# One attention-and-two-MLPs kernel: how the first MLP's input weights are kept, and the order of its opening

## The chip, the cores and the metric

The kernel runs on 1 core of one Trainium2 chip. The metric is the device time of one execution in microseconds (us). Three runs of the kernel before gave 1560.64, 1558.98 and 1560.36 us; the median is 1560.36 us.

## The reference

Two attentions follow each other for each of 8 batches and 8 heads (sequence 576, head dimension 64, 32 packed queries `p`), and then two MLPs work on all 4608 tokens (width 512, hidden width 2048):

```python
p_packed = sm_attn(p, k, v)            # softmax(scale * p k^T) v : 32 rows a head
x = sm_attn(q, p_packed, p_packed)     # 576 rows a head
x = x.transpose(0, 2, 1, 3).reshape(B * S, H * D)          # 4608 x 512
h = x @ w_in;   x = (h * sigmoid(h)) @ w_out               # first MLP (SiLU)
h = x @ w_in2;  x = (h * clip(h + 3, 0, 6) / 6) @ w_out2   # second MLP
```

The weights arrive as float64, q, k, v and p as float32 and the result is float32.

## The kernel before

**Products.** Each fp32 operand of the big products is split into a high word (rounded to the fast fp32r format) and a low word (the rest), and a product is made of three matmuls: high by high, high by low, low by high. A split is two instructions: a rounding copy on ScalarE and a subtraction on VectorE or GpSimd.

**Stages.** The first 512 tokens of a batch make one block, and the last 64 tokens of all eight batches (the "tails") make a ninth. An opening (lines 1567 to 1728, an order written out by hand, function by function) does the attention of batch 0 in two head groups n = 0 and 1, and converts the first weights. Block 0 then runs the first MLP on batch 0 while all of w_in and w_out is converted. Blocks 1 to 7 do the first MLP of the other batches: there w_in is not used itself, but a product of it with the packed values ("fused" weights, `fuse_steps`, L634 to L688). Block 8 runs the first MLP on the tails with w_in itself. After that `Second` does the second MLP.

**Inside a block.** `hidden` (L866 to L872) makes 12 matmuls for one of 16 slices f of the hidden width, then SiLU on ScalarE; `split_g` splits the result (L877 on ScalarE, L878 on VectorE); `project` makes 12 more matmuls two slices later. Between these, a planner (`Plan`) places attention steps and fused products: each has a place (a share of the block), a cost and waiting times, counted in ticks; a matmul is one tick, and in block 0 waiting times are multiplied by 1.5. Each engine and each DMA queue works strictly in the order of the program.

**Conversion of float64 (`conv_a` to `conv_lo`).** A piece of weights (128 x 512 numbers, 512 KB as float64) is loaded to `raw`. `conv_a` (L174, ScalarE) scales the upper half words into a `ring` tile; `conv_b` (L180, ScalarE) scales the lower half words into a second ring tile; `conv_shift` (L189) and `conv_sign` (L193) work on VectorE, `conv_add` (L202) on GpSimd. `conv_hi` (L213, ScalarE) and `conv_lo` (L218, VectorE) split the fp32 value. `Feed` does this for 32 pieces in turn, two for each slice f of block 0; loads in block 0 are issued from ScalarE's queue. The class `Prep` does the same in blocks 1 to 8 for the second MLP's weights (L318 to L336).

**Where w_in goes.** `keep` (L209, SyncE's queue) stores both words of each w_in piece in DRAM (`w1i`, 512 KB a piece, 16 pieces) and the odd pieces of w_out (`w1o`). `next_in` (L241, L243) loads w1i back, 512 KB at a time, 80 times: 64 times for fused products (L645 to L647) and 16 times for block 8. Five tiles `wi` rotate, so a load is issued when the piece five before it has been used.

**Tails of x in block 0.** `step_ut` (L563) transposes the last 64 columns of the weights `d2` on VectorE, `step_xt` (L585) multiplies them, and `flush` stores the result. Both head groups' steps stand in the plan of block 0 at place 0.02, `step_ut` right ahead of its `step_xt`, 12 ticks between the groups.

Of the kernel before, what the change touches and what calls it, by code (L numbers as in the profile page):

```python
# [18 lines left out]
def tile_pack_attention_two_mlps(ctx: ExitStack, tc, q, k, v, p, w_in1, w_out1, w_in2, w_out2, out):  # L19
# [13 lines left out]
    P = 128  # L33
# [93 lines left out]

    GF = T // P
    NG = NF // GF
    w1i = [dram.tile([KC, P, 2, GF, P], F32, name=f"w1i{g}", tag=f"w1i{g}") for g in range(NG)]  # L130
    w1o = {f: dram.tile([2, P, DM], F32, name=f"w1o{f}", tag=f"w1o{f}") for f in range(1, NF, 2)}
    WO = 3
    made = {}
# [40 lines left out]
        nc.scalar.mul(out=r, in_=f32(raw[:, :, 1]), mul=2.0 ** -112)  # L174
        raws[key] = raw, r.bitcast(I32)

    def conv_b(key, room=ring):
        raw, r = raws.pop(key)
        t = room().bitcast(I32)
        nc.scalar.mul(out=t, in_=raw[:, :, 0].bitcast(U32), mul=2.0 ** -29)  # L180
        raws[key] = raw[:, :, 1], r, t

    def conv_begin(key, room=ring):
        conv_a(key, room)
        conv_b(key, room)
# [30 lines left out]
    def conv_lo(key):  # L216
        (kind, f), v, w = key, raws.pop(key), made[key]
        nc.vector.tensor_sub(out=w[:, 1], in0=v, in1=f32(w[:, 0]))  # L218
        if kind == "in":
            kept.append((piece_in(f), f32(w).rearrange("p n (c f) -> p n c f", c=KC)))  # L220
        elif f % 2:
            kept.append((w1o[f].rearrange("n p f -> p n f"), f32(w)))

# [2 lines left out]
        conv_lo(key)  # L226

    def piece_in(f):
        return w1i[f // GF][:, :, :, f % GF, :].rearrange("c p n f -> p n c f")


    want_in, want_out = [], []
    have_in, have_out = {}, {}

    def next_in():
        if want_in:
            key = want_in.pop(0)
            t = wts.tile([P, 2, DM], F32R, tag="wi", name="wi", bufs=5)
            if len(key) == 3:
                j, g, c = key  # L240
                nc.sync.dma_start(out=f32(t).rearrange("p n (i f) -> p n i f", i=GF), in_=w1i[g][c])  # L241
            else:
                nc.sync.dma_start(out=f32(t).rearrange("p n (c f) -> p n c f", c=KC), in_=piece_in(key[1]))  # L243
            have_in[key] = t

    projected = [-1, -1]

# [15 lines left out]
    class Prep:  # L263
# [6 lines left out]
            self.steps = self.all()  # L270

        def room(self):
            return self.pool.tile([P, T], F32, tag="pring", name="pr", bufs=4)

        def load(self, u):

# [302 lines left out]
    def step_xt(n):  # L579
        pf = st.pop(("pp", n))  # L580
        a = st.pop(("a2t", n))
        b = n // QPB
        ps = bank()
        for j in range(2):
            mm(ps[:, j * TAIL:(j + 1) * TAIL], lhsT=pair(pf, j), rhs=a, start=True, stop=True)  # L585
        t = half_kb(n, "xt")[:, 0:2 * TAIL] if n == 1 else at.tile([P, 2 * TAIL], F32, tag="xt", name="xt")
# [49 lines left out]
    def fuse_steps(b, g):  # L636

        ms = mates[b]
        steps = []

        def product(ps, j, qd, first, last):
            lh, ll = [t[:, j * P:(j + 1) * P] for t in st["lp", b, qd]]
            w = have_in[b, g, 2 * qd + j]
            rh, rl = w[:, 0], w[:, 1]
            mm(ps, lhsT=lh, rhs=rh, start=first, stop=False)  # L645
            mm(ps, lhsT=lh, rhs=rl, start=False, stop=False)
            mm(ps, lhsT=ll, rhs=rh, start=False, stop=last)  # L647
# [201 lines left out]

    def hidden(j, f, tick, nxt):  # L850
        if j in (0, B):
            w = made.pop(("in", f)) if j == 0 else have_in[j, f]
            parts = [(w[:, 0, c * P:(c + 1) * P], w[:, 1, c * P:(c + 1) * P], xh[c], xl[c]) for c in range(KC)]
        else:
            s = slice(f % GF * P, (f % GF + 1) * P)
# [707 lines left out]
    beside(load_p, 0)  # L1563
    beside(load_nat, 0, "k", 1)
    load_tail(0, "k")
    load_tail(0, "q")
    beside(load_nat, 1, "k", 0)
    load_p(1)
    load_tail(1, "k")
    load_nat(1, "k", 1)  # L1570
    load_tail(1, "q")
    feed.load()
    for n in range(QPB):
        for j in range(2):
            load_nat(n, "v", j)
        load_tail(n, "v")
        for j in range(2):
            load_nat(n, "q", j)
        if n == 0:
            feed.load()  # L1580
    for _ in range(4):
        feed.load()
    load_p(2)
    load_tail(2, "k")
# [21 lines left out]
    a_qt(0)
    a_kp(1)
    a_qtc(0, "A")
    a_trc("k", 1, 1, "V")
    exp1(0)  # L1610
    a_tr("k", 1, 0)
    a_kpc(1, "V")
    conv_a(unit[0])
    a_tt(0)
    a_trc("k", 1, 0, "V")
    a_t(0)
    a_ttc(0, "A")
    conv_b(unit[0])
    a_s(1, 0)
    a_tc(0, "V")  # L1620
# [10 lines left out]
    a_max(1)
    a_tr("q", 0, 0)
    conv_hi(unit[0])
    a_ppf(0)
    a_tr("q", 0, 1)
    exp1(1)
    a_trc("q", 0, 0, "V")
    a_pt(0)
    a_trc("q", 0, 1, "A")
    post1(1)  # L1640
    a_tt(1)
    a_t(1)
    a_ttc(1, "V")
    a_ptc(0, "A")
    conv_shift(unit[1])
    conv_b(unit[1])
    a_z(0, 0)
    conv_sign(unit[1])
    a_tc(1, "A")
    a_z(0, 1)  # L1650
# [12 lines left out]
    a_tr("q", 1, 1)
    a_trc("q", 1, 0, "A")
    a_ph(0, "V")
    a_pt(1)
    a_trc("q", 1, 1, "A")
    conv_lo(unit[1])
# [62 lines left out]
    for j in range(NBLK):  # L1731
# [112 lines left out]
```

## Time and profile before

| what | value |
| --- | --- |
| median of three runs | 1560.36 us |
| the profiled execution's own time | 1563.44 us |
| its span, first to last instruction | 1561.7 us |
| TensorE busy | 1513.7 us (97%) |
| VectorE, ScalarE, GpSimd busy | 1045.4, 781.2, 193.5 us |
| mean granted TensorE clock | 0.989 of full speed |
| DMA, mean over the span | 230 GB/s |

How to read it: L12 is line 12 of the kernel; PE is TensorE, DVE VectorE, ACT ScalarE, POOL GpSimd, and SPq and ACTq are the queues in which SyncE and ScalarE issue DMAs. In a timeline row the first number is the start, the second the time to the end, both in us; in brackets stands how long the engine had been idle before it, and what released it. TensorE runs at one of two clock levels; a granted clock of 1.00 is 2.4 GHz, one of 0.50 is 1.2 GHz.

### The profile page before, as it was taken

The page shows a single profiled execution, that of the slowest core. Times are in us where ns is not written, and L with a number is a line of the kernel's source. Part 1 is how long each engine was busy: PE and PEld are TensorE (multiplying, and loading weights), DVE is VectorE, ACT ScalarE, POOL GpSimd, SP SyncE. Part 2 cuts the span into 40 slices and gives each one's busy share as a digit, 9 for nine tenths or more (in the row PEclk, how much of TensorE's full clock was granted, in tenths as well). Part 3 has the DMA queues.
Part 4 walks back from the last instruction along what each step waited for, and adds up shares of the span by engine and source line. Part 5 has one row for each costly group of instructions (what it writes and reads, how often), then busy time and mean ns, then how long its engine had stood idle before and what let it go on. Part 6 is the DMA issues. An engine that isn't in the chain of part 4 may idle for free.

```text
span 1561.7 us, 21728 instructions
## 1 busy us (share of the span) xinstructions
PE 1513.7 (97%) x7596; PEld 1234.8 (79%) x7596; DVE 1045.4 (67%) x1673; ACT 781.2 (50%) x1237; POOL 193.5 (12%) x173
## 2 busy tenths in 40 slices
PE   7899999999999999999999999999999999999997
PEld 4666766777777777778878888888888888999997
DVE  6677465755576455663362677877887777878776
ACT  5676545744566546655453334533443344444442
POOL 2333011111120111113132000000000000000000
PEclk9999999999999999999999999999999999999999
DMA  9899786987778776767597667677757776898886
GB/s 241 260 255 316 241 228 169 274 220 194 194 227 215 216 187 183 242 196 227 174 332 213 197 193 244 194 222 223 242 196 216 226 231 202 279 313 254 274 270 201
DMA packets 416460, 358.51 MB, mean 230 GB/s; under 512 B 155232, under 2 KB 307808, under 8 KB 416352
## 3 DMA queue, kind: packets, MB, share of 16 engines
q1 hardware_dynamic: 405552, 343.59, 73.7%
q10 hardware_dynamic: 10800, 13.54, 2.7%
q8 instruction: 61, 1.00, 0.3%
q14 instruction: 47, 0.39, 0.1%
HBM read 295.17 MB, written 61.87 MB: 229 GB/s over the span
## 4 chain that ended last, share of the span: by engine, by line
PE 85%; DMA 4%; DVE 3%; ACT 3%; SPq 2%; issue 1%; POOL 0%; ACTq 0%; POOLq 0%; DVEq 0%
PE acc L885 8%; PE b L1136 7%; PE b L1135 7%; PE b L1137 7%; PE b L1233 7%; PE b L1235 7%; PE b L1236 7%; PE acc L886 7%; PE acc L887 7%; PE hps L862 4%; PE hps L863 4%; PE hps L864 4%; PE abank L645 1%; PE abank L523 1%; PE abank L435 1%
## 5 line engine op out<-in xcount | busy, mean ns | idle before, releaser
L878 DVE TENSOR_TENSOR gl<-hps,gh 128x512 fp32r<-128x512 f32 x144 | 98.9, 687 | 171.5 <-ACT gh L877 170.6
L1235 PE MATMUL b<-ro,ws 128*128 128x512 f32 (+1 forms) x560 | 205.6, 367 | 0.0
L1135 PE MATMUL b<-xc,ws 128*128 128x512 f32 (+1 forms) x560 | 205.6, 367 | 0.0
L1137 PE MATMUL b<-xc,ws 128*128 128x512 f32 (+1 forms) x560 | 205.6, 367 | 0.0
L1136 PE MATMUL b<-xc,ws 128*128 128x512 f32 (+1 forms) x560 | 205.6, 367 | 0.0
L1236 PE MATMUL b<-ro,ws 128*128 128x512 f32 (+1 forms) x560 | 205.5, 367 | 0.0
L1178 DVE TENSOR_TENSOR ro<-g,ro 128x1024 fp32r<-128x1024 f32 (+1 forms) x140 | 161.3, 1157 | 42.7 <-ACT ro L1173 42.3
L1173 ACT CAST ro<-g 128x1024 fp32r<-128x1024 f32 (+1 forms) x140 | 132.9, 969 | 113.4 <-PE b L1233 46.7
L870 ACT ACTIVATE hps<-hps 128x512 f32<-128x512 f32 x144 | 84.0, 583 | 134.2 <-PE hps L864 131.4
L1233 PE MATMUL b<-ro,ws 128*128 128x512 f32 (+1 forms) x560 | 138.2, 368 | 0.6 <-DVE ro L1178 0.4
L885 PE MATMUL acc<-gh,wo 128*128 128x512 f32 x288 | 117.7, 409 | 1.3 <-ACT gh L877 1.3
L885 PE MATMUL acc<-gh,wr 128*128 128x512 f32 x288 | 117.4, 408 | 0.0
L1235 PEld LDWEIGHTS b<-ro,ws 128*128 128x128 f32 x560 | 105.1, 188 | 13.3 <-issue 0.2
L1136 PEld LDWEIGHTS b<-xc,ws 128*128 128x128 f32 x560 | 105.1, 188 | 13.2
L1135 PEld LDWEIGHTS b<-xc,ws 128*128 128x128 f32 x560 | 105.1, 188 | 13.2
L1236 PEld LDWEIGHTS b<-ro,ws 128*128 128x128 f32 x560 | 105.1, 188 | 13.1
L1137 PEld LDWEIGHTS b<-xc,ws 128*128 128x128 f32 x560 | 105.1, 188 | 13.1
L886 PE MATMUL acc<-gl,wo 128*128 128x512 f32 x288 | 114.0, 396 | 0.8 <-DVE gl L878 0.8
L1233 PEld LDWEIGHTS b<-ro,ws 128*128 128x128 f32 x560 | 102.4, 188 | 15.3 <-DVE ro L1178 2.4
L887 PE MATMUL acc<-gh,wo 128*128 128x512 f32 x288 | 113.7, 395 | 0.0
L887 PE MATMUL acc<-gh,wr 128*128 128x512 f32 x288 | 113.6, 394 | 0.0
L886 PE MATMUL acc<-gl,wr 128*128 128x512 f32 x288 | 113.4, 394 | 0.0
(295 smaller groups left out, 2928.4 us busy)
## 6 DMA issues: line engine op xcount, KB each, us to landing
ws<-w2in SPq DMA_DIRECT2D x280, 256.0 KB, 3.2
ws<-w2out SPq DMA_DIRECT2D x280, 256.0 KB, 3.4
wi<-w1i SPq DMA_DIRECT2D x80, 512.0 KB, 5.7
wo<-w1o SPq DMA_DIRECT2D x64, 512.0 KB, 5.5
x1d<-x SPq DMA_DIRECT2D x18, 512.0 KB, 7.1
w1i<-win SPq DMA_DIRECT2D x16, 512.0 KB, 7.4
praw<-in_moe_w_in_dram SPq DMA_DIRECT2D x32, 256.0 KB, 5.7
praw<-in_moe_w_out_dram SPq DMA_DIRECT2D x32, 256.0 KB, 5.2
```

The source lines that it names most:

```text
L878: nc.vector.tensor_sub(out=gl, in0=g, in1=f32(gh))
L885: mm(acc[e], lhsT=w[:, 0, s], rhs=gh, start=first, stop=False)
L886: mm(acc[e], lhsT=w[:, 0, s], rhs=gl, start=False, stop=False)
L887: mm(acc[e], lhsT=w[:, 1, s], rhs=gh, start=False, stop=last)
L1135: mm(ps, lhsT=wh, rhs=xs[k][:, 0, c], start=first, stop=False, skip_group_check=True)
L1136: mm(ps, lhsT=wh, rhs=xs[k][:, 1, c], start=False, stop=False, skip_group_check=True)
L1137: mm(ps, lhsT=wl, rhs=xs[k][:, 0, c], start=False, stop=last, skip_group_check=True)
L1173: nc.scalar.copy(out=t[:, 0], in_=v)
L1178: nc.vector.tensor_sub(out=t[:, 1], in0=self.operand(s), in1=f32(t[:, 0]))
L1233: mm(acc[i], lhsT=wh, rhs=ro[:, 1, f], start=False, stop=last, skip_group_check=True)
L1235: mm(acc[i], lhsT=wh, rhs=ro[:, 0, f], start=first, stop=False, skip_group_check=True)
L1236: mm(acc[i], lhsT=wl, rhs=ro[:, 0, f], start=False, stop=False, skip_group_check=True)
```

## The change

Five edits. (1) w_in pieces are stored unsplit: `w1i` holds one fp32 word for each number, 256 KB a piece. (2) `next_in` loads 256 KB and a new `split_in` splits a loaded tile with a copy on ScalarE and a subtraction on GpSimd, two loads later, or earlier if `piece` asks for it. (3) `conv_b` writes its result over the raw words instead of into a ring tile; `Prep`'s ring has 2 tiles instead of 4. (4) Block 0's tail steps are spread: `step_ut(0)` is the last step of the opening, `step_xt(0)` stands at place 0.05, `step_ut(1)` two (times 1.5) ticks later, `step_xt(1)` 20 (times 1.5) ticks after that, with a `flush` each. (5) The opening's loads and steps are reordered.

```diff
-    w1i = [dram.tile([KC, P, 2, GF, P], F32, ...) for g in range(NG)]
+    w1i = [dram.tile([KC, P, GF, P], F32, ...) for g in range(NG)]
...
-    def conv_b(key, room=ring):
+    def conv_b(key):
         raw, r = raws.pop(key)
-        t = room().bitcast(I32)
-        nc.scalar.mul(out=t, in_=raw[:, :, 0].bitcast(U32), mul=2.0 ** -29)
+        t = raw[:, :, 0]
+        nc.scalar.mul(out=t, in_=t.bitcast(U32), mul=2.0 ** -29)
         raws[key] = raw[:, :, 1], r, t
...
         if kind == "in":
-            kept.append((piece_in(f), f32(w).rearrange("p n (c f) -> p n c f", c=KC)))
+            kept.append((piece_in(f), v.rearrange("p (c f) -> p c f", c=KC)))
...
+    fresh = []
+
+    def split_in(behind):
+        while len(fresh) > behind:
+            t = have_in[fresh.pop(0)]
+            nc.scalar.copy(out=t[:, 0], in_=f32(t[:, 1]))
+            nc.gpsimd.tensor_sub(out=t[:, 1], in0=f32(t[:, 1]), in1=f32(t[:, 0]))

     def next_in():
...
-                nc.sync.dma_start(out=f32(t).rearrange("p n (i f) -> p n i f", i=GF), in_=w1i[g][c])
+                nc.sync.dma_start(out=f32(t[:, 1]).rearrange("p (i f) -> p i f", i=GF), in_=w1i[g][c])
...
             have_in[key] = t
+            fresh.append(key)
+        split_in(2)
+
+    def piece(*key):
+        if key in fresh:
+            split_in(len(fresh) - 1 - fresh.index(key))
+        return have_in[key]
...
-            w = have_in[b, g, 2 * qd + j]          # in fuse_steps
+            w = piece(b, g, 2 * qd + j)
...
-            w = made.pop(("in", f)) if j == 0 else have_in[j, f]          # in hidden
+            w = made.pop(("in", f)) if j == 0 else piece(j, f)
...
     load_tail(0, "k")
-    load_tail(0, "q")
     beside(load_nat, 1, "k", 0)
     load_p(1)
     load_tail(1, "k")
     load_nat(1, "k", 1)
-    load_tail(1, "q")
     feed.load()
     for n in range(QPB):
         for j in range(2):
             load_nat(n, "v", j)
         load_tail(n, "v")
+        load_tail(n, "q")
         for j in range(2):
             load_nat(n, "q", j)
-        if n == 0:
-            feed.load()
-    for _ in range(4):
+    for _ in range(5):
         feed.load()
...
-                plan.add(("xt", n), 0.02, 1, lambda n=n: [step_ut(n), step_xt(n)], [(("xt", m), 8) for m in range(n)], None, 5)
-            plan.add(("flush", 0), 0.02, 0, flush, [(("xt", QPB - 1), 8)])
+                if n:
+                    plan.add(("ut", n), 0.05, 0, lambda n=n: step_ut(n), [(("xt", n - 1), 2)])
+                plan.add(("xt", n), 0.05, 1, lambda n=n: step_xt(n), [(("ut", n), 20), (("flush", n - 1), 10)] if n else [], None, 5)
+                plan.add(("flush", n), 0.05, 0, flush, [(("xt", n), 10)])
```

The opening's new order, one step after the other (each is a function of the kernel before; "A" is ScalarE, "V" VectorE; u0 to u5 are the first six pieces: in0, in1, in2, out0, in3, out1). Before, `conv_a(u1)` stood ahead of `exp1(1)` and `conv_hi(u1)` ahead of `a_zmax(0)`, group 0 was carried through `exp1`, `a_t` and `a_pp` before group 1's scores, `a_sub(0)` was on GpSimd and `a_mul(1)` on VectorE.

```
a_s(1,0) a_trc(k,1,1,A) conv_sign(u0) exp1(0) a_s(1,1) conv_add(u0) post1(0) a_st(1) a_d(1,A) a_tt(0) a_dt(1,A)
conv_hi(u0) a_t(0) a_ttc(0,V) a_max(1) a_qt(0) a_tc(0,A) a_tr(q,0,1) conv_lo(u0) exp1(1) a_pp(0) a_trc(q,0,1,V)
... a_pp(1) a_z(0,1) a_ppf(1) conv_a(u1) conv_b(u1) a_zt(0) ... exp2(0) a_z(1,0) conv_shift(u1) conv_a(u2) a_sum(0)
... conv_a(u3) a_ztc(1) a_zmax(1) conv_a(u4) ... conv_b(u3) a_u(0) exp2(1) ... conv_sign(u1) a_x(0,0) ... conv_lo(u1)
... a_xl(3) conv_b(u4) conv_shift(u2) conv_sign(u2) conv_shift(u3) conv_add(u2) conv_sign(u3) conv_hi(u2) conv_lo(u2) step_ut(0)
```

## Rows read from the trace of the kernel before

**Rows 1.** First part of the page: engine, busy us (share), instructions.
```profile
PE 1513.7 (97%) x7596; PEld 1234.8 (79%) x7596; DVE 1045.4 (67%) x1673; ACT 781.2 (50%) x1237; POOL 193.5 (12%) x173
```

**Rows 2.** Windows view: stretch, length, busy per engine, granted clock, DMA share, GB/s.
```profile
80.00:90.00 10.00, 7.16 (x67) 5.21 (x66) 7.66 (x13) 8.81 (x16) 4.22 (x3) 1.00 0.79 230
...
120.00:140.00 20.00, 16.32 (x106) 12.78 (x105) 13.44 (x25) 14.09 (x28) 5.57 (x5) 0.91 0.98 317
...
800.00:850.00 50.00, 47.87 (x204) 38.89 (x203) 19.69 (x41) 24.12 (x41) 17.78 (x15) 0.97 0.99 294
...
50.00:53.40 3.40, 3.40 (x12) 2.92 (x12) 0.00 (x0) 1.77 (x4) 0.68 (x1) 0.50 0.17 38
...
256.00:336.00 80.00, 73.83 (x399) 53.95 (x398) 53.66 (x103) 50.19 (x87) 12.77 (x14) 0.98 0.84 237
432.00:508.00 76.00, 74.20 (x371) 56.15 (x370) 55.22 (x103) 48.13 (x84) 11.49 (x12) 1.00 0.79 226
```

**Rows 3.** Waits of TensorE, whole run: us in total, times, longest.
```profile
PE abank L507 <- DVE ppf L497: 5.5, 3, 2.3
PE abank L585 <- DVE a2t L563: 5.4, 3, 3.9
```

**Rows 4.** Timeline of the opening: SyncE's queue, ScalarE, TensorE.
```profile
13.04 0.98 SPq L149 DMA_DIRECT2D raw<-in_moe_w_in_dram  x1
...
18.01 0.66 ACT L174 ACTIVATE cr<-raw 128x512 f32<-128x512 f32 x1 [2.65 <-DMA raw<-in_moe_w_in_dram]
...
19.08 0.77 ACT L454 ACTIVATE spare<-spare,s1m 128x576 f32<-128x576 f32 x1
...
38.58 0.40 PE L862 MATMUL hps<-xh,win 128*128 128x512 f32 x1
```

**Rows 5.** Timeline of block 0's first slices: TensorE and VectorE.
```profile
42.18 0.66 PE L585 MATMUL abank<-a2t,ppf 128*128 128x64 f32 x4 [1.36 <-DVE a2t L563]
...
45.46 0.42 DVE L189 TENSOR_SCALAR cr<-cr 128x512 int32<-128x512 int32 x1
...
46.75 1.58 POOL L202 TENSOR_TENSOR cr<-cr 128x512 int32<-128x512 int32 x1 [3.36 <-DVE cr L193]
47.12 1.49 DVE L189 TENSOR_SCALAR cr<-cr 128x512 int32<-128x512 int32 x1
48.65 0.69 DVE L193 SCALAR_TENSOR_TENSOR cr<-raw,cr 128x512 int32<-128x512 int32 x1
...
49.55 0.73 PE L585 MATMUL abank<-a2t,ppf 128*128 128x64 f32 x4 [3.89 <-DVE a2t L563]
```

**Rows 6.** Groups view of 38 to 168 us, ScalarE: count, busy, mean ns, idle before.
```profile
L213 ACT CAST wr<-cr 128x512 fp32r<-128x512 f32 x8 | 5.0, 624 | 2.0 <-DMA w1i<-win 1.5 <-issue 0.4
L213 ACT CAST wo<-cr 128x512 fp32r<-128x512 f32 x8 | 4.9, 616 | 4.1 <-DMA w1o<-wo 2.7 <-DVE cr L193 0.8 <-POOL cr L202 0.6
```

**Rows 7.** Chain of waits in block 0: start, us, what.
```profile
114.21 10.00 DMA w1i<-win
```

**Rows 8.** DMA issues: out, in, queue, count, KB each, median us to landing.
```profile
wi<-w1i SPq DMA_DIRECT2D x80, 512.0 KB, 5.7
...
ws<-w2in SPq DMA_DIRECT2D x280, 256.0 KB, 3.2
```

**Rows 9.** Groups view, whole run, GpSimd: a low-word subtraction.
```profile
L330 POOL TENSOR_TENSOR c<-c,hi 128x640 fp32r<-128x640 f32 x32 | 50.6, 1580 | 0.0
```

**Rows 10.** Timeline at the end of block 1: SyncE's queue and ScalarE.
```profile
267.81 2.01 SPq L241 DMA_DIRECT2D wi<-w1i  x4
...
270.03 0.58 ACT L651 CAST xf<-abank 64x512 fp32r<-64x512 f32 x1
...
274.87 0.58 ACT L870 ACTIVATE hps<-hps 128x512 f32<-128x512 f32 x1
```

**Rows 11.** Timeline in block 8: ScalarE and GpSimd.
```profile
801.78 0.41 ACT L326 CAST hi<-c 128x256 fp32r<-128x256 f32 x1 [5.61 <-POOL c L318]
...
800.46 1.28 POOL L318 TENSOR_TENSOR c<-pr 128x512 int32<-128x512 int32 x1 [9.19 <-DMA w2out<-c]
```

More of the change, by code (lines that the diff above doesn't have):

```diff
@@ L129, in tile_pack_attention_two_mlps @@
     NG = NF // GF
-    w1i = [dram.tile([KC, P, 2, GF, P], F32, name=f"w1i{g}", tag=f"w1i{g}") for g in range(NG)]
+    w1i = [dram.tile([KC, P, GF, P], F32, name=f"w1i{g}", tag=f"w1i{g}") for g in range(NG)]
     w1o = {f: dram.tile([2, P, DM], F32, name=f"w1o{f}", tag=f"w1o{f}") for f in range(1, NF, 2)}
@@ L184, in conv_begin @@
         conv_a(key, room)
-        conv_b(key, room)
+        conv_b(key)
     def conv_shift(key):
@@ L228, in piece_in @@
     def piece_in(f):
-        return w1i[f // GF][:, :, :, f % GF, :].rearrange("c p n f -> p n c f")
+        return w1i[f // GF][:, :, f % GF, :].rearrange("c p f -> p c f")
     want_in, want_out = [], []
     have_in, have_out = {}, {}
+    fresh = []
[4 more added lines that the diff above has]
+            nc.gpsimd.tensor_sub(out=t[:, 1], in0=f32(t[:, 1]), in1=f32(t[:, 0]))
     def next_in():
@@ L240, in next_in @@
                 j, g, c = key
-                nc.sync.dma_start(out=f32(t).rearrange("p n (i f) -> p n i f", i=GF), in_=w1i[g][c])
+                nc.sync.dma_start(out=f32(t[:, 1]).rearrange("p (i f) -> p i f", i=GF), in_=w1i[g][c])
             else:
-                nc.sync.dma_start(out=f32(t).rearrange("p n (c f) -> p n c f", c=KC), in_=piece_in(key[1]))
+                nc.sync.dma_start(out=f32(t[:, 1]).rearrange("p (c f) -> p c f", c=KC), in_=piece_in(key[1]))
             have_in[key] = t
+            fresh.append(key)
[4 more added lines that the diff above has]
+        return have_in[key]
     projected = [-1, -1]
@@ L272, in room @@
         def room(self):
-            return self.pool.tile([P, T], F32, tag="pring", name="pr", bufs=4)
+            return self.pool.tile([P, T], F32, tag="pring", name="pr", bufs=2)
         def load(self, u):
@@ L585, in step_xt @@
             mm(ps[:, j * TAIL:(j + 1) * TAIL], lhsT=pair(pf, j), rhs=a, start=True, stop=True)
-        t = half_kb(n, "xt")[:, 0:2 * TAIL] if n == 1 else at.tile([P, 2 * TAIL], F32, tag="xt", name="xt")
+        t = at.tile([P, 2 * TAIL], F32, tag="xt", name="xt")
         copy_short(out=t, in_=ps[:, 0:2 * TAIL])
@@ L1588, in tile_pack_attention_two_mlps @@
     feed.load()
+    spread_p(0)
     turn_on(AF.Exp)
     a_tr("k", 0, 0)
-    spread_p(0)
+    a_trc("k", 0, 0, "A")
+    a_tr("k", 0, 1)
     a_kp(0)
-    a_trc("k", 0, 0, "V")
-    a_tr("k", 0, 1)
-    a_kpc(0, "V")
+    a_trc("k", 0, 1, "A")
+    a_tr("k", 1, 0)
+    a_kpc(0, "A")
+    spread_p(1)
     a_s(0, 0)
-    a_trc("k", 0, 1, "V")
-    spread_p(1)
+    a_trc("k", 1, 0, "V")
     a_s(0, 1)
+    a_kp(1)
+    a_d(0, "V")
+    conv_a(unit[0])
     a_st(0)
-    a_d(0, "A")
+    a_kpc(1, "A")
@@ L1603, in tile_pack_attention_two_mlps @@
+    conv_shift(unit[0])
     a_tr("k", 1, 1)
     a_dt(0, "A")
+    conv_b(unit[0])
     a_max(0)
[L1606 to L1609, printed above, removed]
+    a_s(1, 0)
+    a_trc("k", 1, 1, "A")
+    conv_sign(unit[0])
     exp1(0)
[L1611 to L1620, printed above, removed]
+    a_s(1, 1)
+    conv_add(unit[0])
     post1(0)
-    conv_shift(unit[0])
@@ L1623, in tile_pack_attention_two_mlps @@
-    a_s(1, 1)
-    conv_sign(unit[0])
     a_st(1)
     a_d(1, "A")
-    conv_add(unit[0])
-    a_pp(0)
-    a_dt(1, "A")
-    conv_a(unit[1])
[L1631 to L1645, printed above, removed]
-    conv_b(unit[1])
[L1647 to L1650, printed above, removed]
@@ L1651, in tile_pack_attention_two_mlps @@
-    conv_lo(unit[0])
-    conv_add(unit[1])
+    a_tt(0)
+    a_dt(1, "A")
+    conv_hi(unit[0])
+    a_t(0)
+    a_ttc(0, "V")
+    a_max(1)
+    a_qt(0)
+    a_tc(0, "A")
+    a_tr("q", 0, 1)
+    conv_lo(unit[0])
+    exp1(1)
+    a_pp(0)
+    a_trc("q", 0, 1, "V")
+    a_qtc(0, "A")
+    a_tt(1)
+    a_ppf(0)
+    a_tr("q", 0, 0)
+    a_ttc(1, "A")
+    post1(1)
+    a_pt(0)
+    a_trc("q", 0, 0, "A")
+    a_ph(0, "V")
+    a_t(1)
+    a_ptc(0, "V")
+    a_pl(0)
+    a_z(0, 0)
+    a_tc(1, "A")
@@ L1653, in tile_pack_attention_two_mlps @@
+    a_pp(1)
+    a_z(0, 1)
+    a_ppf(1)
+    conv_a(unit[1])
+    conv_b(unit[1])
     a_zt(0)
     a_zc(0)
-    a_pp(1)
-    conv_hi(unit[1])
+    a_pt(1)
+    a_tr("q", 1, 1)
     a_ztc(0)
+    a_ptc(1, "A")
     a_zmax(0)
-    conv_a(unit[2])
     a_tr("q", 1, 0)
-    a_ppf(1)
-    a_sub(0, nc.gpsimd)
-    a_tr("q", 1, 1)
+    a_trc("q", 1, 1, "A")
+    a_sub(0, nc.vector)
+    a_qt(1)
     a_trc("q", 1, 0, "A")
[L1665 to L1668, printed above, removed]
@@ L1669, in tile_pack_attention_two_mlps @@
-    a_qt(1)
-    a_ptc(1, "A")
     a_qtc(1, "V")
-    a_pl(0)
     exp2(0)
     a_z(1, 0)
-    conv_shift(unit[2])
-    a_ph(1, "A")
+    conv_shift(unit[1])
+    conv_a(unit[2])
     a_sum(0)
@@ L1679, in tile_pack_attention_two_mlps @@
     conv_b(unit[2])
-    a_pl(1)
-    spread_p(2)
     a_rec(0)
-    conv_a(unit[3])
     a_zt(1)
@@ L1686, in tile_pack_attention_two_mlps @@
     a_zc(1)
+    a_ph(1, "A")
     a_mul(0, nc.gpsimd)
-    conv_b(unit[3])
+    conv_a(unit[3])
     a_ztc(1)
     a_zmax(1)
-    conv_a(unit[5])
+    conv_a(unit[4])
+    a_pl(1)
+    spread_p(2)
     a_sub(1, nc.vector)
-    conv_b(unit[5])
+    conv_b(unit[3])
     a_u(0)
@@ L1700, in tile_pack_attention_two_mlps @@
     a_al(0)
-    conv_a(unit[4])
-    a_mul(1, nc.vector)
+    a_mul(1, nc.gpsimd)
+    conv_a(unit[5])
+    conv_sign(unit[1])
     a_x(0, 0)
+    a_u(1)
     a_x(0, 1)
-    a_u(1)
+    conv_add(unit[1])
     a_xh(0)
+    a_ah(1)
     a_xl(0)
-    a_ah(1)
+    a_al(1)
+    conv_hi(unit[1])
     a_xh(1)
-    a_al(1)
-    conv_b(unit[4])
-    conv_sign(unit[2])
+    conv_lo(unit[1])
     a_x(1, 0)
@@ L1715, in tile_pack_attention_two_mlps @@
     a_x(1, 1)
-    conv_add(unit[2])
     a_xh(2)
@@ L1719, in tile_pack_attention_two_mlps @@
     a_xh(3)
+    conv_b(unit[5])
     a_xl(3)
+    conv_b(unit[4])
+    conv_shift(unit[2])
+    conv_sign(unit[2])
+    conv_shift(unit[3])
+    conv_add(unit[2])
+    conv_sign(unit[3])
     conv_hi(unit[2])
     conv_lo(unit[2])
-    conv_shift(unit[3])
-    conv_sign(unit[3])
+    step_ut(0)
     feed.begun, feed.ended, feed.at = 6, 3, 4
```

## The prediction

> **What bounds the kernel.** I read the first part of the page, then the windows, then TensorE's waits, and then the timeline wherever a window showed TensorE idle. TensorE is busy for 1513.7 us of a span of 1561.7 [rows 1], so 48 us of idle time, and what the lower clock costs, are all that this change can touch: it adds and removes no product of the two MLPs. The reader should see that the loss sits in a few places. One is the opening, ahead of the first product of block 0 at 38.58 [rows 4]. One is block 0: 2.8 us idle in 80 to 90 and 3.7 in 120 to 140, where the granted clock also falls to 0.91 of 20 us, 1.8 us more [rows 2]. One is the stretch 256 to 336, with 6.2 us idle, while 432 to 508 loses only 1.8 [rows 2]. One is block 8, with 2.1 us idle in 800 to 850 and 1.5 us of clock [rows 2]. By name, the waits that the change touches directly are those for the transposed tails, 5.4 us in three, 1.36 and 3.89 of it in block 0 [rows 3, 5]. After the long one the clock stands at 0.50 for 3.4 us, which costs 1.7 us [rows 2].
>
> The sum is made against the profiled execution, 1563.44 us, which is its span and 1.7 us around it. The median of the runs shown, 1560.36, lies 3.1 lower, so 3.1 comes off at the end.
>
> **A, the opening.** ScalarE stands 2.65 us waiting for the second raw piece, issued at 13.04 and in use at 18.01, and group 1's exponential starts only at 19.08 behind it and one rounding copy [rows 4]. In the new order nothing of that piece stands ahead of this exponential; I lay the new chain out (score copies, u0's conversion, exponential of group 0, copy of its transpose) and reach about 16.5, 2.6 us earlier. But the piece's load moves behind all of v and q. With the 5.0 us from issue to use of [rows 4] and an issue near 16.5 it is ready at 21.5, just where ScalarE now wants it, and its two passes still stand ahead of `exp2(0)`. Two q tails leave the front of SyncE's queue, which brings u0 about 1.2 us sooner and leaves q's landing about where it was. I keep 1.6 us of the 2.6: the first product at 37.0. Bounds: 3 us gained, 1 us lost. Moving `a_sub(0)` and `a_mul(1)` between engines lies inside this.
>
> **B, the tails.** `step_ut(1)` went onto VectorE behind a shift of 1.49 us and a sign step of 0.69 [rows 5], and TensorE stood in `step_xt` until it came. With 30 ticks between the two (30 matmuls of 512 columns are 6.4 us at 2.4 GHz, an estimate from the clock) the second wait is gone. For the first: VectorE ends x near 38.5, then come shift, sign, shift beside GpSimd's addition, sign, low word and transposition, 0.42 + 0.69 + 1.49 + 0.69 + 0.7 + 0.2 = 4.2 us (the low word taken like the sign step, the transposition from the end of that step to TensorE's start) [rows 5], so 42.7. TensorE comes to `step_xt(0)` after 21 matmuls, 4.5 us at 2.4 GHz and some gaps, so at 41.8. Of 5.25 us about 1.0 stays: 4.2 gained. A wait of that size left the clock alone before, so the 1.7 us go too. B is -5.9; bounds -7 and 0. What is late next are the pieces in2, out0 and in3; in2's low word is ready about 1.5 us before it is wanted, so I see no new stall at once.
>
> **C, the rest of block 0.** What is lost there is 2.8 + 3.7 + 1.8, and about 1.7 if the clock also falls after the first: 10 us. At its root VectorE is late with `ppf` (two of the three waits in [rows 3]), after ScalarE had waited 1.5 and 2.7 us for stores to free their tiles [rows 6]; one store of w1i took 10 us [rows 7]. These stores halve, 16 times 256 KB less, and the five reloads in block 0 halve too. Against it, TensorE asks for pieces 7.5 us sooner, `raw` is freed by GpSimd's addition instead of VectorE's sign step, and a ring tile is now held until its store lands. Bounds: -10 and +6; I take -3.5, about one of the two waits. The conversion in place takes no instruction away and I cost it at nothing: the strided read on GpSimd is the unknown, hidden while GpSimd is busy 4 to 6 of 10 to 20 us [rows 2]; if GpSimd's additions took half as long again, `conv_hi` would come 0.7 us later, inside C's bounds.
>
> **D, the end of block 1.** Four fused products follow each other and ScalarE has no gap until SiLU at 274.87 [rows 10]. Each step now adds a split: a copy of 0.62 us [rows 6], 2.5 for four. The last two splits want tiles of the four loads issued from 267.81 on [rows 10]; behind the third step's casts and two copies ScalarE comes to the first of them at 271.8. By 3.2 us from issue to landing it is there, by 5.7 it costs 1.7 us [rows 8]; I take 1.5. ScalarE's queue holds SiLU and the copies that free the accumulators behind this, so TensorE waits for all of it: +4.0. Bounds +2.5 and +8 (both waits at full, and a clock drop).
>
> **E, the other reloads.** 60 copies of 0.62 us are 37 us of ScalarE, and 60 subtractions on GpSimd at 512/640 of 1.58 us [rows 9] are 76. ScalarE is busy 63% of those stretches and TensorE idle 5% [rows 2]. If a copy costs TensorE only where it already waits, that is 1.9 us; I take +2. Bounds 0 and +12: a split waits in ScalarE's queue for a tile issued only two steps before, and every SiLU behind it waits too.
>
> **F, block 8.** GpSimd waits 9.19 us for a store to land and ScalarE 5.61 us for GpSimd [rows 11], at 0.99 DMA share [rows 2]. Eleven reloads there halve; against it come 16 copies. I take -1; bounds -3.6 and +3.
>
> Sum: -1.6 - 5.9 - 3.5 + 4.0 + 2.0 - 1.0 = -6.0, so 1557.4, and 1554.3 on the scale of the median.
>
> **The rivals.**
> 1, slower: ScalarE's queue blocks on landings. It decides if a 256 KB reload still takes the 5.7 us that 512 KB took [rows 8], since a tile is split two fused steps after its load is issued, and where the steps come in a bunch, as the four loads in 2 us of [rows 10] show, that is less time than it takes. D becomes 8, E 12, C nothing: -7.5 + 8 + 12 = +12.5, so 1572.9 - 3.1 = 1569.8. For it: the boundary's gapless ScalarE. Against it: 3.2 us for `ws`.
> 2, handed back: block 0 ends when its feed ends. A and B's 7.5 us turn into waits for conversions, so +1.5: 1561.8. For it: ScalarE busy 8.81 and VectorE 7.66 of 10 us [rows 2]. Against it: 14.09 and 13.44 of 20 later.
> 3, the traffic was the root: all of C and F go. -1.6 - 5.9 - 10 + 4 + 2 - 3.6 = -15.1: 1545.2. For it: rows 7 and 11. Against it: ScalarE and VectorE remain loaded.
> 4, GpSimd's added subtractions hold VectorE up. The same shift takes 0.42 us alone and 1.49 beside GpSimd's addition [rows 5], 1.07 more; if VectorE is held up in the critical spot at six of the 80 reloads, 6.4 us: 1560.7. Against it: VectorE has a third of its time free in 256 to 336 [rows 2].
> The Trainium skill, "SBUF — State Buffer", section "SBUF: two separate sides", says that VectorE and GpSimd share one port pair as an exclusive lock, so that some VectorE operations block for a whole GpSimd instruction. The two shifts agree with it; by the rule alone each of the 80 subtractions could block one VectorE operation, and rival 4 would be the forecast.
>
> **Chances.** Forecast 0.48, rival 1 0.12, rival 2 0.17, rival 3 0.15, rival 4 0.08. A measurement of this kernel tells 0.2% (3.1 us) from no change, so faster means under 1557.2 and slower over 1563.5. Faster: 0.46 of the forecast, rival 3 and 0.02 of rival 4, 0.63. Same: 0.02 of the forecast, 0.12 of rival 2, 0.05 of rival 4, 0.19. Slower: rival 1, 0.05 of rival 2, 0.01 of rival 4, 0.18. The range 1543 to 1566 leaves out most of rival 1 and the edges. The likeliest case has 1549 to 1559 for itself.
>
> **What would show it.** A: the first product of block 0 near 37.0. B: no wait for `a2t` over 1.5 us before 60, and no 0.50 clock near 50. C: less idle between 70 and 140, shorter w1i stores. D: SiLU of block 2 some 4 us later after its last fused cast than before. E: idle ScalarE ended by "DMA wi"; none would sink rival 1. F: the clock at 808. The forecast is wrong if block 0 ends less than 5 us earlier than before, or if TensorE waits for `wi` splits in more than a few places.

## The result, and the profile after

The changed kernel takes 1567.75 us (median of 6 runs, 1564.85 to 1570.87) against 1559.67 for the kernel before in the same session. The ratio is 1.0054, 95% interval 1.004 to 1.0068: slower by 0.54%, some 8.4 us. 1554.3 was forecast, within 1543 to 1566; the time lies outside on the slow side. The profiled execution took 1568.68 us, with a span of 1566.9, 5.2 more than before.

The page's first part answers to [rows 1]: ScalarE gained 44 us, GpSimd 108, and VectorE 16.5, although it has four instructions fewer (the new order of the opening moves a few between the engines).

```profile
PE 1512.8 (97%) x7596; PEld 1231.4 (79%) x7596; DVE 1061.9 (68%) x1669; ACT 825.0 (53%) x1321; POOL 301.4 (19%) x253
```

TensorE's waits (us in total, times, longest), beside [rows 3]: the one for the tails' transposition shrank, the one for `ppf` grew, one for q's load stands in the list with 3.1 us, and four for splits are new, 3.7 us in all; the longest of them is shown.

```profile
PE abank L523 <- DVE ppf L513: 8.4, 4, 4.7
...
PE abank L432 <- DMA spare<-in_q_dram: 3.1, 2, 2.3
...
PE abank L601 <- DVE a2t L579: 2.4, 4, 1.8
...
PE hps L878 <- ACT wi L241: 1.7, 1, 1.7
```

The windows of [rows 2]: TensorE is busy for 14.75 us of 120 to 140 instead of 16.32, and for 72.42 of 256 to 336 instead of 73.83, while the DMA shares of these two stretches fell.

```profile
80.00:90.00 10.00, 7.54 (x34) 5.72 (x35) 9.78 (x16) 7.72 (x15) 3.76 (x3) 0.87 1.11 291
120.00:140.00 20.00, 14.75 (x95) 11.26 (x94) 15.98 (x22) 12.01 (x23) 10.85 (x8) 0.91 0.63 165
800.00:850.00 50.00, 46.49 (x200) 36.81 (x199) 24.52 (x43) 26.61 (x47) 28.69 (x22) 1.00 0.82 245
...
256.00:336.00 80.00, 72.42 (x384) 51.91 (x382) 51.52 (x99) 58.02 (x101) 31.72 (x29) 0.96 0.70 182
```

The timeline of the opening, SyncE's queue and TensorE, beside [rows 4]. SyncE issues two v loads at 13.27 and then nothing until 18.12: its next load, the v tail of group 1, needs the tile `vt` (one buffer), and group 0's products read that tile from 17.75. The q loads of group 1 stand behind it, TensorE waits 2.30 us for them, and the first product of block 0 comes at 41.00 instead of 38.58.

```profile
13.27 1.13 SPq L376 DMA_DIRECT2D spare<-in_v_dram  x2
18.12 0.63 SPq L366 DMA_DIRECT2D vt<-in_v_dram  x1
...
19.63 2.63 SPq L387 DMA_DIRECT2D spare<-in_q_dram  x4
...
17.75 0.32 PE L505 MATMUL abank<-vt,a1Tt 64*32 64x64 f32 x8
...
25.64 1.73 PE L432 MATMUL abank<-ident,spare 128*128 128x128 f32 x8 [2.30 <-DMA spare<-in_q_dram]
...
41.00 0.39 PE L878 MATMUL hps<-xh,win 128*128 128x512 f32 x1
```

Despite that start, block 0 is 4.5 us ahead of before at its twelfth slice (SiLU at 123.9 against 128.4). Then it loses all of it: the sixteenth is at 155.6 against 156.0. How large the lead was is uncertain, since single traces scatter: in that of e4 (below), which takes the time of the kernel before, these slices stand at 123.6 and 153.3, and against it the changed kernel goes from 0.3 us behind to 2.3. The timeline of VectorE and GpSimd shows the place, with the shift that takes 0.42 us when alone [rows 5]. Both lines on GpSimd, the new subtraction (L242) and the old addition (L202), have an instruction of VectorE beside them that takes 1.4 to 1.5 us, and the second of these is `ppf`, for which TensorE waits 4.7 us.

```profile
127.25 1.83 POOL L242 TENSOR_TENSOR wi<-wi 128x512 fp32r<-128x512 f32 x1 [1.64 <-ACT wi L241]
...
127.86 1.50 DVE L189 TENSOR_SCALAR cr<-cr 128x512 int32<-128x512 int32 x1
...
130.17 1.28 POOL L202 TENSOR_TENSOR cr<-cr,raw 128x512 int32<-128x512 int32 x1 [1.09 <-DMA raw<-in_moe_w_out_dram]
130.32 1.41 DVE L513 TENSOR_TENSOR ppf<-ppn,mask 128x256 f32<-128x256 f32 x1
```

At the end of block 1, beside [rows 10], four copies of 0.62 us stand between the casts, and SiLU begins at 279.11 instead of 274.87; from block 1's last SiLU that is 24.4 us instead of 21.8. A reload now takes 3.7 us from issue to landing, against 5.7 [rows 8].

```profile
269.20 4.04 SPq L250 DMA_DIRECT2D wi<-w1i  x4
...
270.09 0.62 ACT L241 CAST wi<-wi 128x512 fp32r<-128x512 f32 x1
...
279.11 0.58 ACT L886 ACTIVATE hps<-hps 128x512 f32<-128x512 f32 x1
```
```profile
wi<-w1i SPq DMA_DIRECT2D x80, 256.0 KB, 3.7
```

### The profile page after: what moved, and what is told of

It is laid out like the page before. It is cut to its first block, busy times and chain, and to the rows that moved or that the text cites. A ratio compares the mean times of both kernels' runs of the same rounds, so it can differ in the third digit from the quotient of the medians.

```text
span 1566.9 us, 22022 instructions
## 1 busy us (share of the span) xinstructions
PE 1512.8 (97%) x7596; PEld 1231.4 (79%) x7596; DVE 1061.9 (68%) x1669; ACT 825.0 (53%) x1321; POOL 301.4 (19%) x253
## 4 chain that ended last, share of the span: by engine, by line
PE 79%; ACT 6%; DVE 4%; DMA 4%; issue 3%; SPq 2%; POOL 1%; ACTq 0%; POOLq 0%; DVEq 0%
PE b L1249 7%; PE b L1251 7%; PE b L1252 7%; PE b L1151 7%; PE b L1153 7%; PE b L1152 7%; PE acc L901 7%; PE acc L902 6%; PE acc L903 6%; PE hps L878 4%; PE hps L880 4%; PE hps L879 4%; DMA ws<-w2in 1%; PE abank L451 1%; PE abank L661 1%
## 5 line engine op out<-in xcount | busy, mean ns | idle before, releaser
L242 POOL TENSOR_TENSOR wi<-wi 128x512 fp32r<-128x512 f32 x80 | 107.5, 1348 | 178.6 <-ACT wi L241 164.0
L1232 POOL TENSOR_TENSOR ov<-ov,o 128x1024 f32<-128x1024 f32 (+1 forms) x5 | 10.9, 2182 | 654.6 <-ACT ov L1218 654.6
L901 PE MATMUL acc<-gh,wr 128*128 128x512 f32 x288 | 117.3, 407 | 0.0
L901 PE MATMUL acc<-gh,wo 128*128 128x512 f32 x288 | 116.7, 405 | 0.4 <-ACT gh L893 0.4
```

What stands on the lines that cost most here:

```text
L242: nc.gpsimd.tensor_sub(out=t[:, 1], in0=f32(t[:, 1]), in1=f32(t[:, 0]))
L901: mm(acc[e], lhsT=w[:, 0, s], rhs=gh, start=first, stop=False)
```

## The experiments

Each was timed in five rounds against the kernel before on the same chip; ratios below 1 are faster. Microseconds are the ratio's distance from 1 times 1560. Where the trace times of two variants are compared, the reference is e4, which does the least. Differences of two single traces are good to some microseconds only: e1's last SiLU of block 8 comes 3.5 us ahead of e10's, although by the ratios e1 is 0.8 us slower.

**e1 to e4: one part of the change at a time, on the kernel before.**

```
e1: w1i unsplit, split_in, piece, conv_b in place   (everything else as before)
e2: + step_ut(0) after conv_lo(unit[2]); plan: ("ut", n), ("xt", n), ("flush", n)
e3: the new order of the opening and its loads
e4: conv_b in place, Prep's ring 4 -> 2
```

> The kernel before with the halved stores, the splits at the reload and the in-place low words alone; opening, loads and tails as before. Theory 1 (the splits cost the time): slower by 6 to 10 us, so a ratio near 1.005; SiLU of block 2 begins 3 to 5 us later than before, block 8 ends with another 2 to 4 us more, TensorE has waits ended by ACT wi and POOL wi. Rival (the new opening costs the time and the splits are hidden): within 2 us of before. Rival 3 of the prediction (halved traffic frees block 0): block 1 begins 3 us or more earlier than before.

> The kernel before with only the tails moved: the transposition of group 0's tail stands at the end of the opening, group 1's has a step of its own in the plan. Theory 1 (block 0 ends when its feed ends): 4 to 5 us earlier at block 0's first quarter, then handed back in waits for ppf, block 1 begins within 1 us of before, ratio 0.999 to 1.001. Rival (the feed was held up by the splits, the stores or the in-place low words in the changed kernel, not by its own pace): the 4 to 6 us stay, ratio 0.996 to 0.998.

> The kernel before with only the reordered opening and its loads; the tails are transposed where they were. Theory 1: the first product of block 0 comes 1.5 to 2.5 us later than before, as in the changed kernel, and what is left of it at the start of block 1 is 0 to 2 us, ratio 1.000 to 1.002. Rival (the late opening is made by the in-place low words or their effect on GpSimd): the first product at or before 38.6, as before.

> The kernel before with only the low words converted in place (raw tiles held until GpSimd's addition, half the ring tiles used, the second weights' ring halved). Theory 1: costs nothing, within 1 us of before. Rival (the strided operand slows GpSimd's additions or VectorE beside them): slower by 2 to 5 us, GpSimd's addition of block 0 longer than 1.58 us.

| | ratio | 95% | us |
|---|---|---|---|
| e1, split | 1.0053 | 1.0039 to 1.0066 | +8.3 |
| e2, tails | 0.9957 | 0.9944 to 0.9971 | -6.7 |
| e3, opening | 1.0049 | 1.0030 to 1.0067 | +7.6 |
| e4, in place | 0.9996 | 0.9985 to 1.0007 | -0.6 |

For e1 the splits' theory held in time; by the trace, SiLU of block 2 comes 2.9 us later than before and block 8 adds 1.35, both a little less than it asked for. Its third line, the prediction's rival 3, did not hold: block 1 began only 2.1 us earlier than before, and 0.6 later than in e4. For e2 the rival held: the gain stays, so block 0 is not bound by the pace of its feed. The window from 45 to 55 of e2, and of the kernel before, shows it: TensorE busy throughout at full clock, where it had 6.11 of 10 us at 0.83.

```profile
45.00:55.00 10.00, 10.00 (x49) 7.32 (x47) 9.38 (x14) 8.85 (x19) 5.33 (x4) 1.00 1.07 309
```
```profile
45.00:55.00 10.00, 6.11 (x26) 4.86 (x25) 5.74 (x10) 5.11 (x10) 2.84 (x2) 0.83 0.48 142
```

In e3 the first product came at 40.97, as expected, but I had expected 0 to 2 us to be left of it and 7.6 were. In its trace, that of an execution 5 us slower than its median, the waits for the tails, still in their old place, grew from 5.4 to 7.3 us. It has the same hole in SyncE's queue, 13.35 to 17.71. For e4 theory 1 held: nothing.

**e5 and e6: the opening without SyncE's wait.** e5 is the changed kernel with group 1's v tail in a tile of its own (one of the spares that the change had set free by taking group 1's `xt` out of it); e6 is the same without the reload split.

```
-        if n == 1 and what != "v":
+        if n == 1:
```

> The changed kernel, with one difference: the v tail of group 1 takes a tile of its own instead of waiting for that of group 0, so SyncE no longer stands at it with the loads of q behind it. Theory 1 (the opening is late because of that wait, 13.94 to 18.12 on SyncE): group 1's q lands near 21.5 instead of 25.5, the first product of block 0 comes 3 to 4 us earlier, ratio to the kernel before 1.002 to 1.004. Rival (ScalarE's copies in the new order set the opening): q lands earlier but the first product moves by less than 1 us, ratio 1.005.

> Tails moved, low words in place, new opening with the v tail of group 1 in a tile of its own; the reload split is left out, weights are stored and reloaded split as before. Theory 1: all that the splits cost is gone and the new opening, without SyncE's wait, is as good as the old: 1551 to 1553, ratio 0.994 to 0.997. Rival (the order itself is worse than the old one): 1555 or more, ratio above 0.997.

e5: 1563.03 us, ratio 1.0016 (1.0005 to 1.0028), against 1.0054 of the changed kernel: the wait was worth some 5.9 us, and theory 1 held, if just below its range. The timeline of e5's opening has the loads without a hole and the first product at 36.73.

```profile
12.10 1.13 SPq L376 DMA_DIRECT2D spare<-in_v_dram  x2
13.28 0.63 SPq L366 DMA_DIRECT2D spare<-in_v_dram  x1
13.95 0.62 SPq L366 DMA_DIRECT2D spare<-in_q_dram  x1
14.62 2.63 SPq L387 DMA_DIRECT2D spare<-in_q_dram  x4
...
36.73 0.40 PE L878 MATMUL hps<-xh,win 128*128 128x512 f32 x1
```

e6: 1553.0 us, ratio 0.9953 (0.9937 to 0.9968). That is e2's 0.9957 again: the new order is neither better nor worse in a way these runs can tell, although its first product comes at 36.48. e2 and e6 both beat the kernel before and the changed one.

**e7 and e8: what of the split costs.**

```
e7: -  nc.gpsimd.tensor_sub(out=t[:, 1], in0=f32(t[:, 1]), in1=f32(t[:, 0]))
    +  nc.vector.tensor_sub(out=t[:, 1], in0=f32(t[:, 1]), in1=f32(t[:, 0]))
e8: -  nc.gpsimd.tensor_sub(out=t[:, 1], in0=f32(t[:, 1]), in1=f32(t[:, 0]))
```

> As e1, with the split's subtraction on VectorE instead of GpSimd. Theory 1a (GpSimd's subtraction is the price, by holding VectorE up and by standing in GpSimd's queue ahead of the additions of block 0): ratio 1.000 to 1.003, no wait for wi on GpSimd. Theory 1b (ScalarE's copies, and what waits behind them, are the price): ratio 1.004 to 1.008, as e1 or worse, since 80 subtractions of 0.69 us come onto VectorE, 55 us.

> As e1, without the split's subtraction (the low word of the 80 reloaded tiles is left out of the computation, the products run on the tile as loaded). Theory 1a (the subtraction is the price): 0.998 to 1.002, VectorE's shifts in block 0 at 0.42 us more often, block 0 ends 2 us or more earlier than in e1. Theory 1b (the copies are): ratio 1.004 or more.

e7: 1.0056 (1.0040 to 1.0072). e8: 0.9976 (0.9965 to 0.9987), just below theory 1a's range, with block 0 ending 2.8 us earlier than in e1. The subtraction is worth 0.0077, 12 us, and costs the same on either engine; e7's theory 1a missed: VectorE, busy 1101.1 us there against 1048.8 in e8, has no room for it either. Without it the halved kernel is faster than the one before, copies included.

**e9 to e12: the price taken apart.** All stand on e1. In e12 neither word is computed, and the products read the tile as loaded.

```
e9:  nc.gpsimd.tensor_sub(out=scratch, in0=scratch, in1=scratch)
e10: nc.gpsimd.tensor_sub(out=scratch, in0=f32(t[:, 1]), in1=f32(t[:, 0]))
e11: for c in range(4):   # 128 columns each
         nc.gpsimd.tensor_sub(out=t[:, 1, s], in0=f32(t[:, 1, s]), in1=f32(t[:, 0, s]))
e12: neither copy nor subtraction
```

> As e1, but each of the 80 subtractions on GpSimd takes a tile of constants instead of the reloaded tile, so that it waits for nothing and nobody waits for it; the low word is left out of the computation, as in e8. Theory H (GpSimd's busy time itself costs, because VectorE is held up beside it): VectorE 10 us or more busier than in e8 and the ratio 1.002 to 1.005, against 0.9976 in e8. Rival Q (the price is the waiting: GpSimd's queue behind a subtraction that waits for a landing and a copy, or the products that wait for the low word): 0.997 to 0.999.

> As e1, but the subtraction of the reloaded tile goes into a tile that nobody reads; the products take the tile as loaded. It waits for the landing and the copy as in e1, and no product waits for it. Theory H: within 0.001 of e9. Rival Q, in its first half (GpSimd's queue is blocked by waits): as e1, 1.004 to 1.006, with e9 near e8. Rival Q, in its second half (products wait for the low word): near e8, 0.997 to 0.999, with e9 there too.

> As e1, the subtraction on GpSimd cut into four instructions of 128 columns. If VectorE is held for one whole GpSimd instruction at a time, a held instruction of VectorE loses some 0.3 us instead of 1.1, VectorE is busy 5 to 10 us less than in e1, and the ratio falls to 0.999 to 1.003. If the price is GpSimd's occupied or blocked queue, or VectorE waits through all four pieces, it stays at 1.005 or rises.

> As e1, with neither copy nor subtraction: only the stores and reloads are halved, and the products take the tile as loaded for both words (the split is left out of the computation). The prediction's C and F (halved traffic brings 4.5 us) and e8 (0.9976 with the copies): 0.994 to 0.9975, the difference to e8 being the copies' price, up to 5 us, most of it at the end of block 1. Rival (the copies are hidden): the same as e8 within 0.001.

| on e4, added in turn | ratio | 95% | step, us |
|---|---|---|---|
| e12, stores and reloads halved | 0.9933 | 0.9916 to 0.9951 | -9.8 |
| e8, + ScalarE's copies | 0.9976 | 0.9965 to 0.9987 | +6.7 |
| e9, + GpSimd's subtraction, waiting for nothing | 1.0014 | 1.0002 to 1.0026 | +5.9 |
| e10, + its waits for landing and copy | 1.0048 | 1.0029 to 1.0066 | +5.3 |
| e1, + the products' wait for its result | 1.0053 | 1.0039 to 1.0066 | +0.8 |

The first four steps are larger than their intervals allow for chance; the last isn't. So theory H and the first half of Q hold together, which neither expectation had; e9 lies a little below H's range of 1.002 to 1.005, and e12 below its own. The page's first lines of e8 and e9 show H: VectorE has the work of e8 and one small fill more, and is busy 15.4 us longer.

```profile
PE 1508.1 (97%) x7596; PEld 1230.5 (79%) x7596; DVE 1048.8 (67%) x1673; ACT 823.0 (53%) x1317; POOL 194.7 (13%) x173
```
```profile
PE 1514.0 (97%) x7596; PEld 1234.0 (79%) x7596; DVE 1064.2 (68%) x1674; ACT 823.5 (53%) x1317; POOL 284.7 (18%) x253
```

What that does is seen in the window from 125 to 140, first of e8, then of e9, then of e1. In e8 TensorE waits 2.7 us for `ppf` there; in e9 VectorE comes to it later, the wait is 4.1, and TensorE's clock stays at the half level, 1.2 GHz, for 6.8 us afterwards where it had been 3.4. In e1 it is 4.8 and 6.8. But in the changed kernel 4.7 us of waiting are followed by only 3.4 at the half level, and in e13 (below) 3.5 by none, so the second part of the loss does not follow from the length of the wait alone.

```profile
125.00:140.00 15.00, 12.30 (x51) 9.80 (x50) 10.80 (x19) 10.17 (x22) 5.23 (x5) 0.89 0.81 198
```
```profile
125.00:140.00 15.00, 10.94 (x40) 8.58 (x39) 11.12 (x18) 8.02 (x16) 5.84 (x6) 0.77 0.77 156
```
```profile
125.00:140.00 15.00, 10.23 (x38) 8.11 (x37) 11.14 (x17) 8.06 (x17) 6.50 (x5) 0.77 0.68 152
```

VectorE's timeline, first of e8, then of e9, shows why it comes later. `ppf` itself takes 1.46 us in both, beside the old addition on GpSimd. What differs are a shift and a product ahead of it, which in e9 run beside two of the new subtractions: together 1.3 us more, the difference of the two waits.

```profile
121.32 0.41 DVE L189 TENSOR_SCALAR cr<-cr 128x512 int32<-128x512 int32 x1
...
124.38 0.76 DVE L565 TENSOR_TENSOR d<-d,s2s 128x576 f32<-128x576 f32 x1
...
127.63 1.46 DVE L512 TENSOR_TENSOR ppf<-ppn,mask 128x256 f32<-128x256 f32 x1
```
```profile
121.86 1.26 DVE L191 TENSOR_SCALAR cr<-cr 128x512 int32<-128x512 int32 x1
...
125.76 1.24 DVE L568 TENSOR_TENSOR d<-d,s2s 128x576 f32<-128x576 f32 x1
...
129.50 1.46 DVE L515 TENSOR_TENSOR ppf<-ppn,mask 128x256 f32<-128x256 f32 x1
```

The waits in GpSimd's queue show in e10's timeline, GpSimd and TensorE: two subtractions held up by ScalarE's copies stand ahead of a small product of p (L407), and TensorE waits 1.32 us for that. e9 has no such wait; e1 has it too, 1.2 us. That is 1.3 of the step's 5.3 us. By the two traces e10 falls some 2 us further behind e9 in block 1, where this wait stands, and some 2 in block 8, where TensorE's wait for a copy is 2.4 us instead of 1.5; where the rest arises is not shown.

```profile
179.34 2.64 POOL L244 TENSOR_TENSOR scratch<-wi 128x512 f32<-128x512 f32 x2 [5.66 <-ACT wi L243]
181.94 0.61 POOL L407 TENSOR_TENSOR pbd<-pn,mask 128x256 f32<-128x256 f32 x1
...
182.61 0.44 PE L416 MATMUL abank<-ident,pbd 128*128 128x128 f32 x2 [1.32 <-POOL pbd L407]
```

e11 missed: 1572.35 us, 1.0074 (1.0054 to 1.0094). At 129.5 VectorE's low word did take 0.94 us, where the same one took 1.75 in e1, and in all VectorE was busy 3.7 us less than in e1. But GpSimd took 512 ns for a quarter (its groups view, below), some 2 us for four instead of 1.35, and what waits in or for its queue got later: TensorE's wait for `pbd`, 1.2 us in e1, is 2.0.

```profile
L244 POOL TENSOR_TENSOR wi<-wi 128x128 fp32r<-128x128 f32 x316 | 151.7, 512 | 156.1 <-ACT wi L241 134.6 <-PE abank L485 10.8 <-issue 5.0
```

e12 by its trace: against e4 the halved traffic brings 1.5 us in block 0, some 3 near the end of block 4 and 3.7 in block 8. The middle one is a stall for a copy with the clock's fall behind it, which is gone in e2 too, where the traffic is not halved; I don't count it as shown. In block 8 the fall of the clock, at 807.8 in the trace before and at 804.2 in e4, is gone in e12 and in the changed kernel.

**e13 and e14: how an occupied GpSimd costs, and whether its waits can be taken out.**

```
e13: -  nc.gpsimd.tensor_sub(out=t[:, 1], ...)
     +  for _ in range(2):
     +      nc.gpsimd.memset(scratch, 1.0)
e14: -  split_in(2)        # in next_in
     +  split_in(3)
```

> As e9, but instead of the subtraction of constants GpSimd fills a tile with a constant, twice per reload: it is occupied about as long, and reads nothing; the low word is left out of the computation. Theory H1 (it costs because VectorE is held up while GpSimd reads and writes): VectorE is busy no longer than in e8 (1048.8 us) and the ratio is e8's, 0.996 to 0.999. Theory H2 (it costs because GpSimd's own additions come later): VectorE as in e8, ratio as in e9, 1.000 to 1.003. If VectorE is as busy as in e9 (1064), the fill holds it up as well and the run tells nothing apart.

> As e1, with three unsplit tiles allowed to stand instead of two, so that a split comes one reload later. Theory Q (a split that waits for its landing blocks ScalarE's and GpSimd's queues, about 5 us by e10 against e9): ratio 1.001 to 1.004. Rival (what the queues gain, the products lose, since the split is then done right before its use): 1.005 or more.

e13: 0.9975 (0.9964 to 0.9986), e8's 0.9976 again, as H1 expects. Its first line and its groups view: GpSimd is occupied for 84.5 us by the fills (90.4 by the subtractions in e9), and VectorE is busy 1.4 us longer than in e8, not 15.4. So GpSimd's time alone costs nothing here. What costs 5.9 us in e9 comes with VectorE being held up beside a GpSimd instruction that reads.

```profile
PE 1508.6 (97%) x7596; PEld 1230.4 (79%) x7596; DVE 1050.2 (67%) x1673; ACT 823.2 (53%) x1317; POOL 276.3 (18%) x333
```
```profile
L244 POOL MEMSET scratch<- 128x512 f32 x160 | 84.5, 528 | 7.0
```

The low word of w_out's odd slices on VectorE, both operands in SBUF, in the groups views of e8, e13 and e1: 866 and 853 ns, and 1133 with the subtractions. Its counterpart with one operand in PSUM, the last fence, has 687 ns in e1 and 688 in e8.

```profile
L218 DVE TENSOR_TENSOR wo<-cr,wo 128x512 fp32r<-128x512 f32 x8 | 6.9, 866 | 0.1
```
```profile
L219 DVE TENSOR_TENSOR wo<-cr,wo 128x512 fp32r<-128x512 f32 x8 | 6.8, 853 | 0.0
```
```profile
L218 DVE TENSOR_TENSOR wo<-cr,wo 128x512 fp32r<-128x512 f32 x8 | 9.1, 1133 | 0.3 <-ACT wo L213 0.2
...
L669 DVE TENSOR_TENSOR fused<-abank,fused 64x512 fp32r<-64x512 f32 x48 | 33.0, 687 | 40.5 <-ACT xh L667 13.7 <-ACT xf L667 12.7 <-ACT xl L667 11.3
```

The Trainium skill, "SBUF — State Buffer", section "Who interferes with whom", says that a VectorE instruction with two SBUF inputs contends with a GpSimd instruction that reads SBUF, not with one that only writes it. These three means agree. The low words of w_in's pieces, with the same operands, don't tell the two apart: 773 ns in e8, 833 in e13 and 829 in e9.

e14: 1.0049 (1.0037 to 1.0061). The rival held: what the queues gain, the products lose. By the traces e14 is 2.1 us ahead of e1 when block 8 begins and 2.9 behind at its end. In e14's waits TensorE stands 3.8 us for low words in block 8, against 0.6 in e1.

```profile
PE hps L880 <- POOL wi L242: 3.8, 4, 2.2
```

## Why the prediction was wrong

Point by point, forecast against what the runs gave.

- **A, the opening: -1.6 forecast, wrong.** The first product came 2.4 us later, not 1.6 earlier. The step that failed is the sentence on SyncE's queue, that two q tails leave its front and q's landing stays where it was. It counted the loads ahead of q, and not the tile that one of them needs: `vt` has one buffer, and its reader, group 0's product with v, had moved back in the new order. With that wait out (e5) the first product is at 36.73, where I had put 37.0. The wait costs 5.9 us (e5 against the changed kernel).
- **B, the tails: -5.9 forecast, -6.7 measured (e2).** Right, in mechanism and size, and in e2 it stays gained, which refutes rival 2. In the changed kernel one wait of 1.77 us is left, above the 1.5 I had set as the mark.
- **C and F, halved traffic: -4.5 forecast together, -10.4 measured (e12).** The direction held and the term was too small; rival 3 had 13.6. In block 8 the 3.7 us by the trace exceed F's lower bound of 3.6. For block 0 the trace gives 1.5 of the 3.5.
- **D, the end of block 1: +4.0 forecast,** 2.5 for four copies and 1.5 for a landing. In e8 that is what happens: SiLU of block 2 moves from 270.56 (e12) to 274.62, 4.06 us, and ScalarE waits 1.88 us for a landing in it (below). In the changed kernel's trace no copy waits there, and the boundary is 2.6 us longer than before, near D's lower bound of 2.5.
- **E, the other reloads: +2 forecast. This is the step of the sum that failed.** The copies and the subtraction together cost 18.7 us (e12 to e1); less D's 4.0, 14.7 are E's, above its bound of 12. E worked out the copies only: it names the 76 us of subtractions on GpSimd and gives them no cost. The copies outside D are 2.7, VectorE held up 5.9, waits in GpSimd's queue 5.3, products waiting 0.8.
- **Rival 4** is the mechanism of VectorE's part: priced 6.4, measured 5.9, and given 0.08. That the price is so near is luck as far as the runs go, since six critical reloads were assumed and no run counts them. The point where it went wrong is the argument against it, VectorE's free third in 256 to 336; in 120 to 140, in block 0, VectorE is busy 15.98 of 20 us and TensorE waits for it. Of the 5.1 us by which e9 lies behind e8 at block 8's last SiLU, 3.1 are there when block 0 ends, and 1.6 come in block 8. That most is lost in block 0 is likely and not shown: e13's trace, in which VectorE is hardly held up, lies 3.4 us behind e8's there too, though 1.7 of them are there at the first slice.
- **Rival 1**, ScalarE blocked on landings, isn't the cause: the reloads land in 3.7 us, and by the prediction's own sign, idle ScalarE ended by "DMA wi", it waits 0.5 us in all (2.5 in e1, 2.4 in e8). Its time was also worked out wrong: 12.5 us on the median of 1560.4 are 1572.9, and the prediction takes the 3.1 us off a second time to reach 1569.8.
- **The signs set for the whole:** block 0 ends 0.4 us earlier than before, not the 5 asked for, and TensorE waits for splits in four places, 3.7 us in all.

ScalarE's one wait for a reload in the changed kernel, from its waits (us in total, times, longest), and the landing at the end of block 1 in e8's timeline:

```profile
ACT wi L241 <- DMA wi<-w1i: 0.5, 1, 0.5
```
```profile
269.06 0.62 ACT L241 CAST wi<-wi 128x512 fp32r<-128x512 f32 x1 [1.88 <-DMA wi<-w1i]
```

The parts nearly add up. e1, e2 and SyncE's wait give 8.3 - 6.7 + 5.9 = 7.5 us; measured are 8.4. Not settled is whether the new order gains anything beside that wait: e6 and e2 can't be told apart.

## What to carry to other kernels

A load that is moved waits for its tile's last reader as well as for its place in the queue, and what stands behind it in the queue waits too: look up the reader and how many buffers the tile has. Work for an idle engine is priced by what it does to its neighbours, here VectorE beside a reading GpSimd, and by what its waits put behind them in its own queue, not by its busy share. Look first at the stretch where the neighbour is already what TensorE waits for: there a longer wait came with a longer stretch at the half clock in e9, e10 and e1, though not in the changed kernel.

## What the hardware did that I had not expected

A fill on GpSimd, 528 ns at a time for 84.5 us, lengthened VectorE's work by 1.4 us; a subtraction of about the same total, 90.4 us, by 15.4. Cutting a 512-column subtraction on GpSimd (1347 ns) into quarters of 512 ns made each column dearer by about half: 2048 against 1347 by the means.
